# Tiles of full depth for three small products, and bundles joined, in an attention and feed-forward kernel

## The chip, the cores and the metric

The kernel runs on one core of one Trainium2 chip. The metric is the device time of one execution in microseconds; smaller is better. Each of the core's engines (PE for matrix products, DVE and ACT for work on vectors, POOL as their helper, SP for issuing DMAs) takes its instructions strictly in the order in which the program lists them, and waits at an instruction whose operands are not there.

## The reference

Attention with landmarks (Nystrom), 8 batches, 8 heads, 576 tokens, 64 columns a head, then a feed-forward block whose input is mixed by a Fourier transform:

```python
q_lm = q.reshape(B, H, 32, 18, D).mean(axis=3);  k_lm = the same of k
A, Bm, C = sm(q, k_lm), sm(q_lm, k_lm), sm(q_lm, k)      # sm: softmax of scale * a @ b.T
Z = Bm.T / (norm1(Bm) * norminf(Bm) + 1e-6)
for _ in range(6): Z = 2 * Z - Z @ Bm @ Z
x = heads side by side of A @ Z @ C @ v                   # 576 x 512 a batch
u = x + real(fft(fft(x, axis=1), axis=2))
un = (u - mean) / sqrt(var + 1e-6)                        # over the 512 columns
out = u + relu(un @ w_ch1) @ w_ch2                        # 512 -> 2048 -> 512
```

## The kernel before

The eight heads of a batch stand in two groups of four. The tokens of a batch are four tiles of 128 and a rest of 64, which shares a tile with the rest of the next batch. `attention(b)` writes the work of one batch; `landmarks` in it computes R = C v (32 landmark rows a head), the iteration for Z, and from both the 64 x 32 blocks W (`Wx`) and its transpose (`Wt`); `mix` makes the rows of u from A, W and the Fourier tables. Two tiles of 128 rows of un are a chunk of the feed-forward block: chunks 0 to 3 by `chunk`, the others by `seven`, a scheme with seven block products instead of eight. Numbers that need more than f16 are split into a high and a low f16 part, and a product of two such is three f16 products (`mm3`).

The parts that the change touches, each by its place on PE:

- Last queries' scores. The scores of the 64 rest queries against the landmark keys. They are the third pass (u == 2) of the loop over `aes` in `attention`. `qr[g]` holds the rest queries of group g. Group 0's scores go to PSUM rows 0 to 63 and group 1's to rows 64 to 127, in tiles of 128 x 64 of PE's array (the trace writes such a tile as 128*64: rows of depth * columns).
- Rest tokens. `rest` holds the rest's part of A, high and low, with group 0 in partitions 0 to 63 and group 1 in 64 to 127; it is multiplied by the cosine and sine table `t1t` with a depth of 64, three products a group, two groups side by side in the array (64*128 in the trace). Those six products follow the twelve for the other tokens (`at<-t,mt`) in one bundle, once for cosine and once for sine in each batch.
- Values' product. `values_turned` multiplies C transposed by v for batches from 2 (`LATE`) on; batches 0 and 1 use `values`, which stays as it is. A group has 16 f32 products of depth 128 and 4 of depth 64 in a bundle of its own, with its own PSUM bank. The 64 rows of v's fifth block are loaded twice, to the upper and the lower half of the partitions, and two heads use each half.
- W and its transpose. The transpose (two products, `at<-row,R`) is in one bundle, then its absolute sum `wm` is taken and summed over partitions by a product with `ones` (in `pow2`), and W (eight products, `at<-R,row`) is a second bundle in another bank.

What sets the order: the code doesn't issue instructions; `Order.op` records them with an assumed cost, and `Order.solve` deals them to the engines in simulated time, one list for each engine. PE work between `together()` and `apart()` is a bundle: it stays in one piece. Attention comes ahead of the feed-forward work where its operands are ready, and the feed-forward work fills what is left. PSUM banks and SBUF slots are given out by the same dealing. All instructions carry the line of the one call that issues them, L1307 in the profile, so groups are told apart by the names of tiles: `hp` and `acc` are the feed-forward banks, `at` the banks for everything else (the seven-product scheme also keeps two of them), `big`, `mt`, `ml`, `row`, `sum` and `h` are slots in SBUF.

Of the kernel before, what the change touches and what calls it, by code (L numbers as in the profile page):

```python
# [11 lines left out]
F16 = mybir.dt.float16  # L12
# [4 lines left out]
ALU = mybir.AluOpType  # L17
AX = mybir.AxisListType

P = 128  # L20
# [3 lines left out]
SEG = 73  # L24
# [61 lines left out]
IN_ORDER = ("u", "big", "ml", "mt", "unT", "h", "ws", "sum", "hp", "acc")  # L86
KEEP = ("at", "row")
LINK, PATIENCE = 0.05, 0.0
# [80 lines left out]
class Op:  # L169
    __slots__ = ("engine", "calls", "held", "took", "phase", "group", "margin", "seq", "before", "after", "tiles", "claims", "rank", "start", "end", "nbytes", "port", "name", "other", "urgent")  # L170


class Order:
# [21 lines left out]
    def op(self, engine, held, took, writes, reads, call, nbytes=0, port=False):  # L195
        o = self.bundle if engine == "PE" and self.bundle else None
        if o is None:
            o = Op()
            o.engine, o.calls, o.held, o.took, o.seq = engine, [], 0.0, 0.0, len(self.ops)
            o.phase, o.group, o.margin, o.nbytes, o.port = self.phase, self.group, self.margin, nbytes, port  # L200
            o.other, o.urgent = {}, False
# [12 lines left out]

    def touch(self, o, v, write):
# [19 lines left out]
    def solve(self):  # L235
# [10 lines left out]
        free = dict.fromkeys(engines, 0.0)  # L246
        pipe, port, now, done = 0.0, 0.0, 0.0, []
        self.done = done
# [57 lines left out]
        while events:  # L306
# [22 lines left out]
            for e in [e for e in best if e not in again] + again:  # L329
# [17 lines left out]
                o.start = now  # L347
                free[e] = now + o.held
                if o.port:
# [71 lines left out]
class Kernel:  # L421
# [95 lines left out]
    def mm(self, out, a, b, start=True, stop=True, share=1.0):  # L517
        n, m = math.prod(b.shape[1:]), math.prod(a.shape[1:])
        if a.dtype != F32:
            held = max(0.02, 0.003 + n / 2400 * share + (0.01 if share < 1.0 or 100 < n < 200 else 0.0))  # L520
        else:
            held = max(0.2, 0.02 + 4 * n / 2400) * (m / 128 if m < 128 else 1.0) * share
        self.order.op(
            "PE", held * self.cold, 0.2, [out], [a, b],
            (self.nc.tensor, "matmul", (out, a, b), {"start": start, "stop": stop, "skip_group_check": True}),
        )
        self.order.ops[-1].name = "mm"

    def tr(self, out, a, ident):
        self.order.op("PE", 0.21 * self.cold, 0.2, [out], [a, ident], (self.nc.tensor, "transpose", (out, a, ident), {}))  # L530
        self.order.ops[-1].name = "tr"

    def mm3(self, out, a, b, start=True, stop=True, share=1.0):
# [124 lines left out]
    def attention(self, b):  # L658
# [9 lines left out]
        NQ = 16 * SEG  # L668
# [33 lines left out]
        qm = [h[:, 0:2048].rearrange("p (y r t) -> p y r t", y=2, r=2) for h in qhs]  # L702
        qr = [h[:, 2048:2304].rearrange("p (y r t) -> p y r t", y=2, r=2) for h in qhs]
        for g in range(2):
            qs = loads[g][1][:, 0:NQ].rearrange("p (x t) -> p x t", t=2 * SEG)
            for t, a, w in ((qm[g], 1, 128), (qr[g], 129, 16)):
                split(
                    *(t[:, y].rearrange("p r (s t) -> p (r s) t", t=w) for y in range(2)),
                    qs[:, :, a : a + w], sc[:, g : g + 1],
                )  # L710
# [9 lines left out]
        for u in range(3):  # L720
# [4 lines left out]
            self.together()  # L725
            for j in range(4) if u < 2 else range(2):
                rows, at, g = (slice(0, P), 128 * j, u) if u < 2 else (slice(64 * j, 64 * j + 64), 0, j)
                for pr in range(2):
                    mm3(ps[rows, at : at + 128].rearrange("p (h r m) -> p h r m", h=2, r=2)[:, :, pr],
                        lambda y: qm[g][:, y, pr, 128 * j : 128 * j + 128] if u < 2 else qr[g][:, y, pr],  # L730
                        lambda y: kbd[:, g, y, pr, :])
            self.apart()
# [13 lines left out]
        for u in range(3):  # L746
# [4 lines left out]
            av = ae.rearrange("p (h m) -> p h m", m=32)  # L751
            if u == 2:
                rest = self.small([P, 2, 128], "rest", F16, bufs=1)
# [3 lines left out]
            else:  # L757
                self.A.copy(hy[:, :, 0], av)
                self.E.tensor_tensor(hy[:, :, 1], av, hy[:, :, 0], ALU.subtract)
            self.turn(AT, hl)  # L760
            ATs.append(AT)
            if u == 2:
                Fs.append(rest)
                break
# [13 lines left out]
        for x in range(2):  # L778
# [124 lines left out]
    def values_turned(self, loads, T, ci, R):  # L903
        V, mm = self.V, self.mm
        ET = self.big()[:, 0 : 2 * S]
        for a, b in ((0, 640), (640, 2 * S)):
            self.E.tensor_tensor(ET[:, a:b], T[:, a:b], T[:, 2 * S + a : 2 * S + b], ALU.add)
        E = ET.rearrange("p (c m) -> p c m", m=P)
        low, high = slice(0, 64), slice(64, P)
        for g in range(2):  # L910
            vf = loads[g][2].rearrange("p (c d) -> p c d", c=5)
            ps = self.at()
            self.together()
            tiles = [(0, low, 4, 4)] + [(x, slice(0, P), 5 * x + c, c) for c in range(4) for x in range(2)] + [(1, high, 4, 4)]
            for x, rows, blk, c in tiles:
                for r in range(2):
                    i, at = 2 * r + x, 64 * g + 32 * r
                    mm(ps[32 * i : 32 * i + 32, 0:64], E[rows, blk, at : at + 32], vf[rows, c, 64 * i : 64 * i + 64],
                       (x, c) in ((0, 4), (1, 0)), (x, c) in ((0, 3), (1, 4)))
            self.apart()  # L920
            V.tensor_scalar(R[:, g], ps[:, 0:64], ci[:, g : g + 1], 2.0**-14, ALU.mult, ALU.mult)

    def landmarks(self, b, loads, qbd, lm):
# [73 lines left out]
        for g in range(2):  # L997
# [3 lines left out]
            )  # L1001
        pst = self.at()
# [3 lines left out]
        self.apart()  # L1006
        self.order.ops[-1].before.update(self.used[1])
        self.used[1] = {}
        wm = small(1, "wm")
        V.tensor_reduce(wm, pst[:, 0:128], AX.X, ALU.add, apply_absolute_value=True)  # L1010
        count = len(self.order.ops)
        ew, rw = self.pow2(wm, 1, "wx")
        total = self.order.ops[count]
        total.urgent = True
        ps = self.at()
        self.together()
        for g in range(2):
# [5 lines left out]
        self.apart()  # L1023
        self.order.ops[-1].before[total] = None
        self.order.ops[-1].before.update(self.used[0])
        self.used[0] = {}
        sc = small(3, "scw")
# [3 lines left out]
        Wx, Wt = self.Wx, self.Wt  # L1031
        for W, src in ((Wt, pst[:, 0:128]), (Wx, ps[:, 0:256])):
            self.split(*(W[:, y].rearrange("p a b -> p (a b)") for y in range(2)), src, sc[:, 0:1])
# [341 lines left out]
```

## Time and profile before

| | us |
|---|---|
| median of 3 runs | 965.05 (964.23 to 967.74) |
| the profiled execution | 965.58 |
| its span | 963.4 |
| PE busy | 911.0 (95%), 10510 matmuls |
| DVE, ACT, POOL busy | 760.1, 482.8, 216.5 |
| mean granted clock of PE | 0.979 |

A row of the timeline gives the start, the duration and the count of instructions of one kind in a row; matmuls overlap, so the time a row takes on PE is the difference of two starts. Each f32 product stands as two records. Shapes of a matmul are tile of the array, output, type: `64*32 64x64 f32` is a depth of 64 and 32 columns of the array, 64 columns streamed. A bracket at the end of a row is the idle time ahead of it and who ended it.

### The profile page before, as it was taken

Reading aid. Unit: us, or ns where it says so; the run is one execution under the profiler, and the core shown is the slowest. Engines: PE = TensorE matmul, PEld = TensorE weight load, DVE = VectorE, ACT = ScalarE, POOL = GpSimd, SP = SyncE. Lnnn points to the kernel's source line nnn. Section 1 sums busy time; section 2 is a strip of 40 time slices with the busy share of each in tenths; the row PEclk is TensorE's granted clock in tenths of the full one; section 3 lists DMA queues with packets and bytes.
Section 4 is the critical chain, followed back from the end, with each engine's and each line's share of the span. In section 5 each row is a group of like instructions: output and inputs, shape, how many; then the busy total and the mean of one; then the engine's idle time right before and its main releaser. Section 6 shows DMA issues by size and latency. Waiting matters only on the chain. (4 is left out here: it accounts for less than half of the span.)

```text
span 963.4 us, 26055 instructions
## 1 busy us (share of the span) xinstructions
PE 911.0 (95%) x10510; PEld 731.0 (76%) x10510; DVE 760.1 (79%) x2016; ACT 482.8 (50%) x1007; POOL 216.5 (22%) x250
## 2 busy tenths in 40 slices
PE   5767999999999999999999999999999999999997
PEld 3546667666666788888887778887888878888886
DVE  7989996898898769887789886996698858665455
ACT  5999842355455445454454444545345533333332
POOL 0211210153643213321223002242031303101010
PEclk9768999999999999999999999999999999999999
DMA  9966110734737433556252733467235522435231
GB/s 350 355 226 178 41 37 13 182 105 95 258 90 189 157 89 104 155 124 213 67 155 88 195 104 89 133 130 216 67 100 154 132 74 73 120 112 117 82 105 50
DMA packets 161993, 128.23 MB, mean 133 GB/s; under 512 B 80080, under 2 KB 150736, under 8 KB 161744
## 3 DMA queue, kind: packets, MB, share of 16 engines
q1 hardware_dynamic: 161872, 126.57, 45.3%
q8 instruction: 82, 1.34, 0.6%
q14 instruction: 39, 0.32, 0.1%
HBM read 94.15 MB, written 14.68 MB: 113 GB/s over the span
## 5 line engine op out<-in xcount | busy, mean ns | idle before, releaser
L1307 PE MATMUL hp<-unT,w 128*128 128x256 f16 x3264 | 388.5, 273 | 10.3 <-DMA unT<-row 8.9
L1307 PEld LDWEIGHTS <-w 128*128 128x128 f16 (+1 forms) x3584 | 345.0, 99 | 68.5 <-issue 10.4
L1307 PEld LDWEIGHTS <-h 128*128 128x128 f16 x2604 | 247.2, 98 | 61.9 <-issue 6.6
L1307 PE MATMUL acc<-w,h 128*128 128x256 f16 (+1 forms) x1260 | 198.6, 294 | 1.1 <-DVE u L1307 0.4
L1307 DVE TENSOR_TENSOR sum<-ws 128x256 f32<-128x256 f32 (+1 forms) x278 | 99.8, 405 | 69.9 <-ACT ws L1307 68.1
L1307 ACT ACTIVATE ws<-hp 128x512 f32<-128x512 f32 x112 | 66.6, 595 | 140.1 <-PE hp L1307 139.9
L1307 ACT CAST h<-sum 128x640 f16<-128x640 f32 x112 | 81.1, 724 | 82.6 <-DVE sum L1307 68.1
L1307 PE MATMUL at<-big,h 128*128 128x256 f16 x672 | 110.1, 273 | 0.0
L1307 POOL TENSOR_TENSOR sum<-ws 128x256 f32<-128x256 f32 (+1 forms) x58 | 41.3, 727 | 252.9 <-ACT ws L1307 197.9
L1307 DVE TENSOR_TENSOR h<-sum,h 128x640 f16<-128x640 f32 x79 | 65.0, 823 | 19.2 <-ACT h L1307 18.0
L1307 POOL TENSOR_TENSOR h<-sum,h 128x640 f16<-128x640 f32 x33 | 46.4, 1405 | 150.3 <-ACT h L1307 150.3
L1307 ACT CAST row<-row 128x256 f16<-128x256 f32 (+1 forms) x76 | 36.7, 505 | 40.4 <-DVE row L1307 32.2
L1307 DVE TENSOR_REDUCE lm<-big 128x32 f32<-128x576 f32 (+1 forms) x48 | 44.3, 946 | 14.7 <-DMA big<-k_dram 8.1
L1307 PE MATMUL at<-w,h 128*128 128x256 f16 x336 | 55.0, 273 | 0.0
L1307 PE MATMUL acc<-big,h 128*128 128x256 f16 x336 | 55.0, 273 | 0.0
L1307 PEld LDWEIGHTS <-big 128*128 128x128 f16 (+1 forms) x768 | 40.8, 104 | 11.0 <-issue 5.0
L1307 ACT CAST h<-ws 128x256 f16<-128x256 f32 x112 | 45.3, 404 | 2.7
L1307 DVE SCALAR_TENSOR_TENSOR u<-at,scw,row 128x128 f32<-128x128 f32 (+3 forms) x120 | 39.0, 386 | 3.7 <-PE at L1307 3.5
L1307 DVE TENSOR_TENSOR h<-ws,h 128x256 f16<-128x256 f32 x95 | 40.5, 426 | 0.0
L1307 ACT ACTIVATE big<-big 128x1168 f16<-128x1168 f32 (+1 forms) x26 | 25.3, 983 | 29.2 <-DMA big<-q_dram 21.7
L1307 PEld LDWEIGHTS <-mt 64*128 64x128 f16 (+1 forms) x752 | 28.6, 98 | 14.5 <-issue 8.0
L1307 DVE SCALAR_TENSOR_TENSOR u<-acc,winv,u 128x512 f32<-128x512 f32 x50 | 35.3, 741 | 3.0 <-PE acc L1307 2.7
(223 smaller groups left out, 1254.7 us busy)
## 6 DMA issues: line engine op xcount, KB each, us to landing
big<-sums SPq DMA_DIRECT2D x336, 128.0 KB, 2.2
w<-w_dram SPq DMA_DIRECT2D x22, 512.0 KB, 8.1
big<-q_dram SPq DMA_DIRECT2D x16, 584.0 KB, 6.2
big<-k_dram SPq DMA_DIRECT2D x16, 576.0 KB, 4.8
out_dram<-u SPq DMA_DIRECT2D x36, 256.0 KB, 2.2
big<-v_dram SPq DMA_DIRECT2D x12, 512.0 KB, 4.8
big<-w_dram SPq DMA_DIRECT2D x10, 512.0 KB, 6.5
sums<-row SPq DMA_DIRECT2D x40, 128.0 KB, 2.5
```

The lines of the kernel that those rows point to most:

```text
L1307: getattr(engine, name)(*map(real, args), **{k: real(x) for k, x in kw.items()})
```

## The change

Four edits to products, and one to the planner:

1. Last queries' scores: `qr` gets twice the columns, with group g's queries in its own half of 64 and zeros in the other (16 memsets on POOL in all). Both groups' products then use the full 128 x 128 tile and are summed in the same PSUM rows.
2. Rest tokens: `rest` holds, for a group, the high part in one half of the partitions and the low part in the other, and `t1t` holds the same rows in both halves; two products of depth 128 a group take the place of three of depth 64. On ACT two copies become one cast and four copies of 64 partitions.
3. Values' product: both groups in one bundle and one bank, 40 products, all of depth 128. The fifth block of v is loaded by columns: the heads of one parity have their 64 rows in the upper partitions, the other in the lower, and zeros beside them, which the padded input holds. That is three DMAs a group for it instead of two.
4. W and its transpose: one bundle, one bank; the absolute sum is taken behind both.
5. The planner adds 0.095 (`SWITCH`) to PE's assumed time where the tile of the array changes, and assumes less for narrow f32 products. This changes the order alone.

```diff
+    def mode(self, mode):
+        o = self.ops[-1]
+        if o.modes and o.modes[-1] != mode:
+            o.held += SWITCH
+            o.took += SWITCH
+        o.modes.append(mode)
...
-                for x in range(2):
-                    self.dma(to[64 * x : 64 * x + 64, 4], src[0:64, 4])
+                of = lambda t, x: t[:, 4].rearrange("p (r x d) -> p r x d", r=2, x=2)[:, :, x]
+                self.dma(of(to, 0), of(src, 0))
+                for half in range(2):
+                    self.dma(of(to, 1)[64 * half : 64 * half + 64], of(src, 1)[64 - 64 * half : 128 - 64 * half])
...
+            self.G.memset(qr[g][..., 64 - 64 * g : 128 - 64 * g], 0.0)
...
-                rows, at, g = (slice(0, P), 128 * j, u) if u < 2 else (slice(64 * j, 64 * j + 64), 0, j)
+                    at, g = (128 * j, u) if u < 2 else (0, j)
...
-                self.A.copy(rest[:, 0], ae)
-                self.E.tensor_tensor(rest[:, 1], ae, rest[:, 0], ALU.subtract)
-                self.A.copy(hy, rest.rearrange("p y (h m) -> p h y m", m=32))
+            self.A.copy(hy[:, :, 0], av)
+            self.E.tensor_tensor(hy[:, :, 1], av, hy[:, :, 0], ALU.subtract)
...
+                    self.A.copy(rest[own, g], hy[own, :, 0])
+                    self.A.copy(rest[other, g], hy[own, :, 1])
...
-            for ya, yb in ((0, 0), (0, 1), (1, 0)):
-                for g in range(2):
-                    rows = slice(64 * g, 64 * g + 64)
-                    mm(pss[g][:, 0:320], Fs[2][rows, ya], self.t1t[rows, x, yb, :], False, ya == 1, 0.5)
+            for g in range(2):
+                for y in range(2):
+                    mm(pss[g][:, 0:320], Fs[2][:, g], self.t1t[:, x, y, :], False, y == 1)
...
+        for c in range(5):
+            for g in range(2):
+                for i in range(4):
+                    at = 64 * g + 32 * (i // 2)
+                    blk = c if c == 4 else 5 * (i % 2) + c
+                    mm(ps[32 * i : 32 * i + 32, 64 * g : 64 * g + 64], E[:, blk, at : at + 32], vf[g][:, c, 64 * i : 64 * i + 64],
+                       c == 0 and g == 0, c == 4)
...
-            mm(pst[64 * g : 64 * g + 64, 0:128], R[:, g], nbd[:, g, :, 0:32])
-        self.apart()
...
+            mm(pst[64 * g : 64 * g + 64], R[:, g], nbd[:, g, :, 0:32])
         for g in range(2):
             for i in range(4):
```

The built lists show it. On PE, the values' product of batch 2 before: behind a step of the iteration (`ES`), a bundle for each group (`big`, the slots of C transposed and v; `at`, two banks):

```order
L1307 LDWEIGHTS w_110
L1307 MATMUL hp_106<-big_69,w_110 128x256
L1307 MATMUL at_105<-ES_165 32x64 x8
L1307 MATMUL at_103<-big_64,big_67 32x64 x20
L1307 MATMUL at_104<-big_65,big_67 32x64 x20
L1307 LDWEIGHTS sum_100
L1307 MATMUL acc_108<-w_111,sum_100 128x512
```

And after, its last rows (ten rows of four, two groups by turns, into one bank):

```order
L1319 MATMUL at_105<-big_66,big_65 32x64 x4
L1319 MATMUL at_105<-big_64,big_65 32x64 x4
L1319 MATMUL at_105<-big_66,big_65 32x64 x4
L1319 LDWEIGHTS h_94
L1319 MATMUL acc_108<-w_111,h_94 128x512
```

The two bundles of 20 have become one of 40, away from the iteration's step and between products of the feed-forward block.

On PE, W in batch 0 before, where `acc_108<-w_110` is a product of the weights with themselves that the kernel uses for scales:

```order
L1307 LDWEIGHTS w_110
L1307 MATMUL acc_108<-w_110 128x128
L1307 MATMUL at_103<-row_82,R_139 64x128 x2
L1307 MATMUL at_104<-wm_166,ones 128x1
L1307 MATMUL at_105<-R_139,row_82 64x64 x8
```

After:

```order
L1319 MATMUL at_103<-wm_204,ones 128x1
L1319 LDWEIGHTS w_110
L1319 MATMUL acc_108<-w_110 128x128
L1319 MATMUL at_102<-row_82,R_139 64x128 x2
L1319 MATMUL at_102<-R_139,row_82 64x64 x8
L1319 MATMUL at_104<-wm_166,ones 128x1
```

The sum `wm_166` has moved behind both products, which now share a bank.

On ACT in batch 0, the copies of the rest before (`ae`, the rest's part of A; `hl`, what is sent to be transposed; `w` and `ws`, weights being split):

```order
L1307 ACTIVATE w_110<-w_111 128x512 x2
L1307 CAST rest_184<-ae_178 128x128
L1307 ACTIVATE w_110<-w_111 128x512
L1307 CAST mt_74<-mt_78 128x512
L1307 COPY hl_182<-rest_184 128x256
L1307 ACTIVATE w_110<-w_111 128x512 x3
L1307 ACTIVATE Wt<-at_103,scw_172 128x128
L1307 CAST mt_78<-mt_75 128x512
L1307 ACTIVATE Wx<-at_105,scw_172 128x256
```

After:

```order
L1319 ACTIVATE w_110<-w_111 128x512 x3
L1319 CAST hl_182<-ae_178 128x4x32
L1319 CAST mt_74<-mt_78 128x512
L1319 COPY rest_184<-hl_182 64x128 x4
L1319 ACTIVATE w_110<-w_111 128x512 x3
L1319 CAST mt_78<-mt_75 128x512
L1319 ACTIVATE ws_97<-w_110,wsa 128x512
L1319 ACTIVATE Wt<-at_102,scw_172 128x128
L1319 ACTIVATE Wx<-at_102,scw_172 128x256
```

Four short copies have come in, and a step of the weights stands ahead of W's split. Further down, three more weight steps (`ACTIVATE w`) stand ahead of the first row's cast for the feed-forward block than before.

More of the change, by code (lines that the diff above doesn't have):

```diff
@@ L86 @@
 IN_ORDER = ("u", "big", "ml", "mt", "unT", "h", "ws", "sum", "hp", "acc")
-KEEP = ("at", "row")
+KEEP, SWITCH = ("at", "row"), 0.095
 LINK, PATIENCE = 0.05, 0.0
@@ L169 @@
 class Op:
-    __slots__ = ("engine", "calls", "held", "took", "phase", "group", "margin", "seq", "before", "after", "tiles", "claims", "rank", "start", "end", "nbytes", "port", "name", "other", "urgent")
+    __slots__ = ("engine", "calls", "held", "took", "phase", "group", "margin", "seq", "before", "after", "tiles", "claims", "rank", "start", "end", "nbytes", "port", "name", "other", "urgent", "modes")
 class Order:
@@ L246, in solve @@
         free = dict.fromkeys(engines, 0.0)
-        pipe, port, now, done = 0.0, 0.0, 0.0, []
+        pipe, port, now, done, mode = 0.0, 0.0, 0.0, [], None
         self.done = done
@@ L347, in solve @@
                 o.start = now
+                if o.modes:
+                    if o.modes[0] != mode:
+                        o.held += SWITCH
+                        o.took += SWITCH
+                    mode = o.modes[-1]
                 free[e] = now + o.held
@@ L526, in mm @@
         )
+        size = lambda v: 128 if v > 64 else 64 if v > 32 else 32
+        self.order.mode((size(a.ap.ap[0][1]), size(m)))
         self.order.ops[-1].name = "mm"
@@ L531, in tr @@
         self.order.ops[-1].name = "tr"
+        self.order.mode((128 if a.ap.ap[0][1] > 64 else 64, 128))
     def mm3(self, out, a, b, start=True, stop=True, share=1.0):
@@ L725, in attention @@
             self.together()
[L726 to L729 removed]
+            for pr in range(2):
+                for j in range(4) if u < 2 else range(2):
+                    at, g = (128 * j, u) if u < 2 else (0, j)
+                    mm3(ps[:, at : at + 128].rearrange("p (h r m) -> p h r m", h=2, r=2)[:, :, pr],
                         lambda y: qm[g][:, y, pr, 128 * j : 128 * j + 128] if u < 2 else qr[g][:, y, pr],
[L731 removed]
+                        lambda y: kbd[:, g, y, pr, :], u < 2 or j == 0, u < 2 or j == 1)
             self.apart()
@@ L762, in attention @@
             if u == 2:
-                Fs.append(rest)
+                rest = self.small([P, 2, 4, 32], "rest", F16, bufs=1)
+                for g in range(2):
+                    own, other = (slice(64 * i, 64 * i + 64) for i in (g, 1 - g))
+                    self.A.copy(rest[own, g], hy[own, :, 0])
+                    self.A.copy(rest[other, g], hy[own, :, 1])
+                Fs.append(rest.rearrange("p g h m -> p g (h m)"))
                 break
@@ L908, in values_turned @@
         E = ET.rearrange("p (c m) -> p c m", m=P)
-        low, high = slice(0, 64), slice(64, P)
-        for g in range(2):
[L911 to L919, printed above, removed]
-            self.apart()
-            V.tensor_scalar(R[:, g], ps[:, 0:64], ci[:, g : g + 1], 2.0**-14, ALU.mult, ALU.mult)
+        vf = [loads[g][2].rearrange("p (c d) -> p c d", c=5) for g in range(2)]
+        ps = self.at()
+        self.together()
+        for c in range(5):
+            for g in range(2):
+                for i in range(4):
[3 more added lines that the diff above has]
+                       c == 0 and g == 0, c == 4)
+        self.apart()
+        for g in range(2):
+            V.tensor_scalar(R[:, g], ps[:, 64 * g : 64 * g + 64], ci[:, g : g + 1], 2.0**-14, ALU.mult, ALU.mult)
     def landmarks(self, b, loads, qbd, lm):
@@ L1001, in landmarks @@
             )
-        pst = self.at()
+        ps = self.at()
+        pst = ps[:, 256:384]
         self.together()
         for g in range(2):
-            mm(pst[64 * g : 64 * g + 64, 0:128], R[:, g], nbd[:, g, :, 0:32])
[L1006 to L1016, printed above, removed]
+            mm(pst[64 * g : 64 * g + 64], R[:, g], nbd[:, g, :, 0:32])
         for g in range(2):
@@ L1023, in landmarks @@
         self.apart()
-        self.order.ops[-1].before[total] = None
-        self.order.ops[-1].before.update(self.used[0])
-        self.used[0] = {}
+        for used in self.used:
+            self.order.ops[-1].before.update(used)
+            used.clear()
+        wm = small(1, "wm")
+        V.tensor_reduce(wm, pst, AX.X, ALU.add, apply_absolute_value=True)
+        count = len(self.order.ops)
+        ew, rw = self.pow2(wm, 1, "wx")
+        self.order.ops[count].urgent = True
         sc = small(3, "scw")
```

21 lines of the change are left out of this document (8 added, 13 removed).

## The prediction

> **What bounds the kernel now.** I read the page first, then the windows of the span, then TensorE's waits, then its timeline where the change falls.
>
> ```profile
> PE 911.0 (95%) x10510; PEld 731.0 (76%) x10510; DVE 760.1 (79%) x2016; ACT 482.8 (50%) x1007; POOL 216.5 (22%) x250
> PE   5767999999999999999999999999999999999997
> PEclk9768999999999999999999999999999999999999
> ```
>
> TensorE (PE) is busy 911.0 of 963.4 us; from the fifth slice on nothing but nines, at the full granted clock. Windows (busy us of PE, PEld, DVE, ACT, POOL; clock, DMA share, GB/s):
>
> ```profile
> 0.00:50.00 50.00, 30.68 (x439) 21.35 (x440) 42.55 (x134) 38.44 (x83) 6.31 (x12) 0.86 1.04 355
> 50.00:100.00 50.00, 35.16 (x366) 29.25 (x364) 45.01 (x102) 48.09 (x94) 6.91 (x8) 0.76 0.63 198
> 300.00:500.00 200.00, 200.00 (x2407) 167.28 (x2405) 160.95 (x428) 96.29 (x199) 52.69 (x60) 1.00 0.46 131
> 500.00:700.00 200.00, 193.97 (x2426) 162.54 (x2425) 159.65 (x429) 93.65 (x198) 48.50 (x54) 1.00 0.47 132
> ```
>
> In the first 100 us PE stands idle for 34 us, because ACT and DVE are nearly full (48.09 and 45.01 of 50). Later it hardly stands, because matmuls of the feed-forward layer fill every hole of the attention. So there a microsecond of PE work removed is a microsecond of the end, and a microsecond added to ACT, DVE, POOL or SP costs nothing unless PE, which takes its instructions in order, stands for it. The waits that do exist (total, times, longest):
>
> ```profile
> PE hp L1307 <- DMA unT<-row: 8.9, 1, 8.9
> PE at L1307 <- DVE big L1307: 5.1, 5, 2.7
> ```
>
> **What a change of tile costs.** Three products of 256 columns, the same again, then a product in 32x32 tiles, on PE's timeline (start, us):
>
> ```profile
> 409.99 0.49 PE L1307 MATMUL at<-big,h 128*128 128x256 f16 x3
> 410.31 0.49 PE L1307 MATMUL at<-w,h 128*128 128x256 f16 x3
> 410.74 0.33 PE L1307 MATMUL at<-ES 32*32 32x32 f32 x16
> ```
>
> From start to start three take 0.32 us (0.108 each) when the next row keeps the 128x128 tile, and 0.43 when it doesn't. So a change into a smaller tile costs about 0.10 us. The way out shows at the rest tokens:
>
> ```profile
> 661.06 0.99 PE L1307 MATMUL at<-t,mt 128*128 128x160 f16 x12
> 661.99 0.58 PE L1307 MATMUL at<-t1t,rest 64*128 64x320 f16 x6
> 662.50 1.49 PE L1307 MATMUL hp<-unT,w 128*128 128x256 f16 x12
> ...
> 110.03 1.47 PE L1307 MATMUL acc<-w,mt 128*128 128x512 f16 x6
> 111.34 0.38 PE L1307 MATMUL at<-nrm,ones_bd 128*128 128x128 f32 x2
> ```
>
> Products of 160 columns take (0.93 - 0.10) / 12 = 0.069, of 256 columns 0.108, of 512 columns 1.31 / 6 = 0.218: one line, 0.426 ns a column, so 320 columns are 0.136. The six half-depth products run as three pairs, 0.41; the row takes 0.51, so the way out costs 0.10 too. The Trainium skill has this (TensorEngine Tiling (Array Packing), Key Properties: changing the tiling mode drains the engine) without a price; the trace gives it, 0.10.
>
> **The parts on PE.**
>
> Rest tokens, 16 bundles (8 batches, cosine and sine). Before 0.10 + 0.51 = 0.61. After, 4 x 0.136 = 0.545 and no change of tile, since the products before them have 128x128 tiles. Gain 0.065 x 16 = 1.0 us; an error of 0.01 a product moves it by 0.6, so 0.4 to 1.7. This is where the skill speaks against the change: the same page (Theoretical Speedup) gives a depth of 64 or less up to twice the rate in two row tiles. By that alone, three pair times become four, and this part would lose 16 x 0.136 = 2.2 us; the time would be 961.6. The pairs do show in the row (0.51 for six); the two changes around them, 0.20, take it back.
>
> Last queries' scores, 8 bundles of 12 (the first row pair is the other queries', 24 products of the same columns in the full tile):
>
> ```profile
> 733.35 0.86 PE L1307 MATMUL at<-kbd,big 128*128 128x64 f16 x24
> 734.05 0.49 PE L1307 MATMUL at<-w,h 128*128 128x256 f16 x3
> ...
> 740.87 0.47 PE L1307 MATMUL at<-kbd,big 128*64 128x64 f16 x12
> 741.27 0.94 PE L1307 MATMUL hp<-unT,w 128*128 128x256 f16 x7
> ```
>
> Full tile: 0.70 / 24 = 0.029 each, so 12 x 0.029 = 0.35 against 0.10 + 0.40. Gain 0.15 x 8 = 1.2; 0.8 if half of them stand beside another small tile, where one change stays.
>
> Values' product, batches 2 to 7 (each f32 product is two records; the last row is batch 1's older form, 16 products of full depth and 4 of half; the row after it, at 110.03, stands above):
>
> ```profile
> 664.19 1.95 PE L1307 MATMUL at<-big,big 64*32 64x64 f32 x80 [0.21 <-DVE big L1307]
> 666.07 1.16 PE L1307 MATMUL hp<-unT,w 128*128 128x256 f16 x9
> ...
> 552.62 1.12 PE L1307 MATMUL at<-big,big 64*32 64x64 f32 x40
> 553.67 0.50 PE L1307 MATMUL at<-big,h 128*128 128x256 f16 x3
> ...
> 109.20 0.90 PE L1307 MATMUL at<-big,ml 128*32 128x64 f32 x40
> ```
>
> Both groups in a row take 1.88 with four changes inside and one at the end, plus 0.10 ahead: 1.98 a batch. A group alone takes 1.05 + 0.10, two of them 2.30. In the order, four batches have them in a row and two apart. After: 40 products, one change ahead, one behind. Price of one, from the pair: (1.88 - 0.50) / 40 = 0.0345; from batch 1: (0.83 - 0.20) / 20 = 0.0315. The second is nearer in shape; 40 of them and 0.20 are 1.46, by the first 1.58. I take 1.5: gain 4 x 0.48 + 2 x 0.80 = 3.5 us (3.0 to 3.8).
>
> W and its transpose, 8 batches:
>
> ```profile
> 560.13 0.44 PE L1307 MATMUL at<-row,R 128*64 128x128 f32 x4
> 560.50 0.83 PE L1307 MATMUL acc<-w,h 128*128 128x256 f16 x6
> ...
> 565.09 0.74 PE L1307 MATMUL at<-R,row 128*64 128x64 f32 x16 [0.67 <-DVE wx_e L1307]
> 565.76 0.50 PE L1307 MATMUL acc<-w,h 128*128 128x256 f16 x3
> ```
>
> 0.37 and 0.67, each with a change on both sides. In one bundle a way in and a way out go: 0.20 x 8 = 1.6; 1.5, since one stood beside another small tile; at least 1.2.
>
> Sum on PE: 1.0 + 1.2 + 3.5 + 1.5 = 7.2 us (ends 5.4 to 8.3). A count checks it: walking through the tiles of both built programs I find 373 changes of tile before and 283 after. 90 x 0.10 = 9.0, less the longer rest products (16 x (0.545 - 0.41) = 2.2) and scores (8 x 0.05 = 0.4), plus the values' shorter ones (6 x 40 x 0.003 = 0.7): 7.1.
>
> **What it adds elsewhere.** ACT: two copies a batch become one cast and four copies of 64 partitions. Nearest rows, and the weight steps that now stand ahead:
>
> ```profile
> 32.17 0.20 ACT L1307 COPY ES<-at 128x64 f32<-128x64 f32 x1
> 33.96 0.28 ACT L1307 CAST rest<-ae 128x128 f16<-128x128 f32 x1
> 36.10 0.40 ACT L1307 COPY hl<-rest 128x256 f16<-128x256 f16 x1
> 36.41 1.79 ACT L1307 ACTIVATE w<-w 128x512 int32<-128x512 uint32 x3
> ```
>
> Four at 0.20 to 0.28 and one at 0.28, less 0.28 and 0.40: 0.4 to 0.7 more a batch. From batch 1 on ACT is half idle (93.65 of 200) and PE has the feed-forward work to go on with: nothing. In batch 0 ACT is full and PE waits 8.9 us for the first unT, so it counts there: 0.6. Also, three more weight steps (1.8 us) come ahead of the first row's cast in the new order; they are only moved, so the loss is between nothing and 1.8. I take none of it, since the weights finish that much sooner and the first chunk needs both; the end is 0.6 + 1.8 = 2.4.
>
> W's absolute sum now follows the 8 products of Wx too, 0.67 later; its scales and both splits wait behind it, and the product with t2 for them. PE fills that with the cosine and sine products or the feed-forward: nothing. If that cover failed, 0.67 a batch. The bundle also waits for the last product with the old Wx, which stands ahead of it on PE anyway.
>
> DMA and POOL: the values' fifth block comes in three pieces instead of two, 12 issues more on SP (the memset of the unused half of the last queries is 16 more on POOL, which is busy 48.5 of 200).
>
> ```profile
> L1307 SPq DMA_DIRECT2D big<-v_dram x40: 379/527/1376, 3.8 to 734.5; - x40
> ```
>
> At 0.527 us an issue a batch's SP queue is 1.1 us longer; what stands behind are sums units and transposes. The DMA engines are busy 0.46 of the time: nothing; uncovered, 1.1 in six batches.
>
> The order: the planner now counts 0.095 for a change of tile, so PE's row is dealt anew nearly everywhere. That removes no work. Its price is waits, below.
>
> Forecast: 7.2 - 0.6 = 6.6 us. The profiled execution took 965.58 (span 963.4 and 2.2 around it), 0.5 above the median of the three runs, 965.05. 965.05 - 6.6 = 958.4.
>
> **Rivals.** A measurement of this kernel tells about 0.5%, 4.8 us, from no change: 960.2 to 969.9.
>
> 1. The waits at the merged places go too. The 5.1 us of waits for DVE big stand there: the values' rows (0.21 above, and two longer ones) and this one, W's transpose behind a DVE that waits for a load:
>
> ```profile
> 671.02 1.42 DVE L1307 TENSOR_REDUCE lm<-big 128x32 f32<-128x576 f32 x2 [2.73 <-DMA big<-q_dram]
> ...
> 675.02 0.44 PE L1307 MATMUL at<-row,R 128*64 128x128 f32 x4 [2.74 <-DVE big L1307]
> ```
>
> If all go, 958.4 - 5.1 = 953.3. For it: a new order, with changes of tile counted. Against: a load that is late stays late.
>
> 2. The first chunk starts late. From the first unT on, PE is full, so its delay comes one for one. The three weight steps and the four copies, with the DVE work that waits for them, could make it 5 us instead of 0.6: 962.8. It is "no change" from 2.4 us on and slower only past 12. For it: ACT's 48.09 of 50. Against: the moved work returns.
>
> 3. Slower: the new order sets attention products on PE closer to what DVE makes, and PE, in order, stands like at 675 us. A wait of that kind is 2.74; five more than now (13.7) turn it into 972.1, and slower is decided from 11.5 us, between four and five. For it: such waits exist, and loads are still issued by one SP queue. Against: from 300 to 700 us only 6.0 are idle (200.00 and 193.97 of 200 in the windows), and PE has feed-forward rows to hand.
>
> 4. Weight loads are exposed. The fuller tiles load 128 rows where half-depth tiles could load beside each other.
>
> ```profile
> L1307 PEld LDWEIGHTS <-w 128*128 128x128 f16 (+1 forms) x3584 | 345.0, 99 | 68.5 <-issue 10.4
> ```
>
> 64 rest and 96 score products with 0.099 each in the open would be 15.8 us: 974.2. Against: 24 full-tile scores take 0.70, 0.029 each, loads included. The Trainium skill (TensorE: Matmul & The Clock Gate, Part 3) states that a weight load overlaps with running matmuls only when its row group differs; by that rule this rival would come, and the scores' row speaks against it.
>
> That the change doesn't do what it says is settled by the order: the bundles are merged, 90 changes fewer. Only their price could fail, and it shows in three rows.
>
> **How the numbers follow.** Forecast (955.5 to 960.2): 0.50. Rival 1: 0.14. Rival 2: 0.24. Rival 3: 0.10. Rival 4: 0.02. Faster by over 0.5%: 0.50 + 0.14 = 0.64; within: 0.24; slower: 0.12. The range reaches down to where the best sum meets rival 1 (965.05 - 8.3 - 5.1 = 951.7) and up to rival 2 with one new wait (962.8 + 2.74 = 965.5) and a part of rival 3: 952 to 967. Outside stay most of rivals 3 and 4 and the far end of 1, under 0.2.
>
> **What the new profile would show.** Right: PE busy about 7 us less; the rest tokens as 128*128 128x320 rows, four in 0.55; one values' row a batch of 80 records in about 1.4 to the next row; scores at 0.03 each in one form; W's two shapes side by side; the first feed-forward row at 77 to 78 us. Wrong: rest products well over 0.14, or 64-column ones over 0.04 (rival 4); the wait for unT past 11 us (rival 2); PE's waits for DVE big, ES, mt or row grown by over 5 us after 172 us (rival 3).

## Result, and the profile after

The change made the kernel slower. It took 977.81 us (median of 4 runs, 974.57 to 981.8); the kernel before took 964.64 on the same chip. The ratio, over undisturbed runs only and so not quite the quotient of the medians, is 1.0115 (95% interval 1.0081 to 1.015). I had forecast 958.4. The profiled execution took 974.57, with a span of 972.8. It is the fastest of the four, at a mean granted clock of 0.973 against 0.967 to 0.971 in the others; so the profile shows some 9 of the 13 us between the medians.

Engines, PE by slice and the granted clock by slice, from the page of the kernel after:

```profile
PE 908.0 (93%) x10478; PEld 734.3 (75%) x10478; DVE 768.7 (79%) x2022; ACT 488.2 (50%) x1031; POOL 221.4 (23%) x260
PE   4666899999999999999999899999999999999997
PEclk9767999999999999999999999999999999999999
```

PE is busy 3.0 us less, and the span is 9.4 longer: PE stands more. The windows tell where (same columns as before):

```profile
0.00:50.00 50.00, 26.76 (x424) 19.68 (x424) 42.28 (x130) 37.66 (x82) 4.82 (x12) 0.83 1.03 352
50.00:100.00 50.00, 34.70 (x366) 27.03 (x344) 45.06 (x108) 46.99 (x93) 8.76 (x11) 0.73 0.59 189
100.00:172.00 72.00, 68.31 (x801) 44.75 (x799) 58.40 (x175) 38.47 (x85) 14.74 (x15) 0.98 0.09 26
300.00:500.00 200.00, 196.62 (x2361) 164.26 (x2359) 160.63 (x431) 96.04 (x205) 43.26 (x49) 1.00 0.50 131
500.00:700.00 200.00, 193.87 (x2404) 164.57 (x2402) 168.80 (x444) 94.85 (x203) 52.86 (x59) 1.00 0.48 132
```

The third window of the kernel before:

```profile
100.00:172.00 72.00, 70.65 (x826) 45.14 (x825) 60.84 (x181) 35.91 (x79) 11.61 (x12) 1.00 0.07 18
```

Where nothing stood between 300 and 500 us, 3.4 us stand now. Ahead of 172 us PE is busy 6.7 us less (3.9, 0.5 and 2.3 in the three windows), at a lower clock in each.

The products themselves cost what was forecast, or less. PE's timeline after: rest tokens, last queries' scores, W and its transpose, values, each with the row behind it:

```profile
150.94 0.71 PE L1319 MATMUL at<-t1t,rest 128*128 128x320 f16 x4
151.48 0.99 PE L1319 MATMUL at<-t,mt 128*128 128x160 f16 x12
...
135.26 0.52 PE L1319 MATMUL at<-kbd,big 128*128 128x64 f16 x12
135.62 1.46 PE L1319 MATMUL acc<-w,h 128*128 128x512 f16 x6
...
139.60 0.44 PE L1319 MATMUL at<-row,R 128*64 128x128 f32 x4
139.87 0.70 PE L1319 MATMUL at<-R,row 128*64 128x64 f32 x16
140.50 1.47 PE L1319 MATMUL acc<-w,h 128*128 128x512 f16 x6
...
660.12 1.32 PE L1319 MATMUL at<-big,big 128*32 128x64 f32 x80
661.37 0.50 PE L1319 MATMUL acc<-w,h 128*128 128x256 f16 x3
```

From start to start: 0.54 (0.61 before), 0.36 (0.50), 0.90 for W's two (0.37 + 0.67 and one change of tile more), and 1.25 for both groups' values (1.88, or 2.10 apart).

To see the rest I use one number of my own, **standing time**: the clock time at a point of the trace, less the full-clock work of PE's row up to there. The work is the sum, over the row, of what each kind of product takes from start to start in the two traces (by tile, type, columns and the row behind it, after 180 us). Standing time so holds waits and half-clock time. Work is 885.3 us before and 880.6 after. Standing by a given time, us:

| | 100 | 172 | 350 | 800 | 945 |
|---|---|---|---|---|---|
| before | 53.7 | 54.8 | 62.1 | 71.8 | 71.6 |
| after | 57.0 | 62.7 | 75.1 | 86.2 | 85.9 |

So 4.7 us of work went and 14.3 of standing came: 7.9 by 172 us, 5.1 more by 350, 1.4 more to 800. The split hangs on how the kinds are formed. Formed by the shapes of a product and of the next one, with starts behind a wait left out, work is 888.0 before and 881.1 after: 6.9 went and 16.4 came. Both counts agree on where it came.

### The profile page after: what moved, and what is told of

The parts are those of the page before. It is cut to its first block, busy times and chain, and to the rows that moved or that the text cites. A ratio compares the mean times of both kernels' runs of the same rounds, so it can differ in the third digit from the quotient of the medians.

```text
span 972.8 us, 26055 instructions
## 1 busy us (share of the span) xinstructions
PE 908.0 (93%) x10478; PEld 734.3 (75%) x10478; DVE 768.7 (79%) x2022; ACT 488.2 (50%) x1031; POOL 221.4 (23%) x260
## 4 chain that ended last, share of the span: by engine, by line
PE 65%; DVE 15%; ACT 7%; DMA 6%; issue 4%; POOL 2%; SPq 1%; DVEq 0%; ACTq 0%; POOLq 0%
PE hp L1319 29%; PE at L1319 19%; PE acc L1319 16%; DMA big<-big 2%; DVE row L1319 2%; DVE u L1319 2%; DMA big<-q_dram 2%; ACT w L1319 2%; DVE h L1319 1%; DVE mt L1319 1%; ACT row L1319 1%; DVE big L1319 1%; ACT h L1319 1%; ACT big L1319 1%; ACT ws L1319 1%
## 5 line engine op out<-in xcount | busy, mean ns | idle before, releaser
L1319 DVE TENSOR_TENSOR sum<-ws 128x256 f32<-128x256 f32 (+1 forms) x277 | 104.0, 421 | 72.6 <-ACT ws L1319 69.9
L1319 POOL TENSOR_TENSOR sum<-ws 128x256 f32<-128x256 f32 (+1 forms) x59 | 43.4, 750 | 288.8 <-ACT ws L1319 225.9
L1319 ACT CAST row<-row 128x512 f16<-128x512 f32 (+1 forms) x76 | 36.8, 505 | 38.3 <-DVE row L1319 25.0
L1319 DVE SCALAR_TENSOR_TENSOR row<-at,scw,row 128x262 f32<-128x262 f32 (+1 forms) x48 | 21.6, 485 | 20.0 <-ACT row L1319 19.7
```

The lines of the kernel that those rows point to most:

```text
L1319: getattr(engine, name)(*map(real, args), **{k: real(x) for k, x in kw.items()})
```

## Experiments

Each of the five sets below was timed on a chip of its own, in 3 rounds against the kernel before. Its median was 965.1, 966.5, 965.6, 966.7 and 966.4 us there and 964.6 beside the changed kernel, so a difference across sets can be off by up to 2 us. The kernels hold the old and the new version of each part, and a line of numbers says from which batch on the new one counts (99: never). PLAN stands for the cost of a change of tile, HELD for the new price of narrow f32 products; up to e7 HELD goes with PLAN. PRICE multiplies the attention products' prices from batch 2 on. "Sum" is the planner's own total for PE. The values' edit exists from batch 2 on alone, in the changed kernel too. Results together (time: median; standing by 172 us, from 172 to 800, from 800 to 945). Standing is that of the profiled execution, which in after, e10, e17 and e18 was 2 to 3 us faster than the median:

| run | edits from batch | costs | sum | us | ratio, interval | standing |
|---|---|---|---|---|---|---|
| before | none | old | 913.6 | 965 | | 54.8, 17.0, -0.2 |
| after | 0 | new | 925.4 | 977.8 | 1.0115, 1.0081 to 1.015 | 62.7, 23.5, -0.3 |
| e1 | 0 | old | 914.8 | 967.8 | 1.0025, 1.001 to 1.004 | 57.3, 23.2, -0.1 |
| e2 | none | new | 932.5 | 974.9 | 1.0104, 1.0069 to 1.0139 | 57.6, 23.9, -0.2 |
| e3 | 2 | new from 2 | 923.4 | 967.9 | 1.0022, 1.0006 to 1.0039 | 56.3, 23.5, -0.3 |
| e4 | 2 | old | 914.5 | 957.8 | 0.9918, 0.9892 to 0.9944 | 56.3, 13.7, -0.3 |
| e5 | 2, rests 0 | old | 914.8 | 962.5 | 0.995, 0.9933 to 0.9967 | 57.1, 17.5, -0.3 |
| e6 | 2, scores 0 | old | 914.5 | 958.1 | 0.9915, 0.9893 to 0.9937 | 56.7, 13.8, -0.3 |
| e7 | 2, W 0 | old | 914.5 | 962.4 | 0.9961, 0.9948 to 0.9974 | 54.7, 18.2, -0.2 |
| e8 | 2 | change of tile from 2 | 934.2 | 966.2 | 0.9999, 0.9987 to 1.0012 | 55.7, 23.9, -0.3 |
| e9 | 2 | the same, PRICE 0.832 | 914.8 | 953.4 | 0.9864, 0.9843 to 0.9884 | 55.5, 10.0, 0.0 |
| e10 | 2 | old, PRICE 1.168 | 934.2 | 971.5 | 1.0051, 1.0032 to 1.0069 | 55.4, 25.5, -0.2 |
| e11 | 2 | narrow f32 from 2 | 903.5 | 953.0 | 0.9857, 0.9836 to 0.9878 | 56.1, 9.7, 0.2 |
| e12 | 2 | old, margin 2.2 | 914.5 | 969.5 | 1.0036, 1.0018 to 1.0053 | 56.3, 24.0, 0.5 |
| e13 | 0 | old, PRICE 0.906 | 903.7 | 966.2 | 0.9989, 0.9973 to 1.0004 | 57.3, 11.1, 10.0 |
| e14 | 2 | old, margin 1.8 | 914.5 | 963.0 | 0.9962, 0.9944 to 0.998 | 56.3, 17.8, -0.2 |
| e15 | none | old, PRICE 0.906 | 902.6 | 973.6 | 1.0063, 1.0042 to 1.0085 | 56.5, 23.7, 0.2 |
| e16 | 2 | old, PRICE 0.906 | 903.4 | 961.9 | 0.9941, 0.9921 to 0.9961 | 57.0, 11.0, 5.9 |
| e17 | 0 | old, PRICE 0.906 in 2 to 4 | 909.3 | 964.5 | 0.998, 0.9963 to 0.9997 | 59.2, 15.3, -0.1 |
| e18 | 0 | new, PRICE 0.832 | 907.4 | 972.0 | 1.0053, 1.0032 to 1.0074 | 62.2, 18.4, -0.1 |

The work is 879.2 to 880.6 in every kernel with the edits, and 884.6 to 885.3 in every one without. Nearly all the rest is the order.

**First set: the edits against the costs.** The line of numbers, e1 to e4:

```diff
-SCORES, RESTS, VALUES, WS, PLAN = 0, 0, 2, 0, 0       # the changed kernel
+SCORES, RESTS, VALUES, WS, PLAN = 0, 0, 2, 0, 99      # e1
+SCORES, RESTS, VALUES, WS, PLAN = 99, 99, 99, 99, 0   # e2
+SCORES, RESTS, VALUES, WS, PLAN = 2, 2, 2, 2, 2       # e3
+SCORES, RESTS, VALUES, WS, PLAN = 2, 2, 2, 2, 99      # e4
```

> The four edits with the planner's old costs (no 0.095 for a change of tile). 278 changes of tile instead of 373 before. Theory A (the new costs deal a worse order, the edits themselves gain): about 959, PE's waits as before. Theory B (the edits in batch 0 make the first chunk late and the rest follows): 970 to 978, first unT wait ends past 80 us. Theory C (any new dealing of the early part loses, whatever caused it): also 968 to 980, with idle PE time in the first 150 us some 5 us more than before.

> The planner's new costs alone, no edit to any product (371 changes of tile). Theory A: 972 to 982, slower than with the edits by the 5 to 7 us that they gain. Theory B: 965, as before. Theory C: 968 to 980, with more idle PE time in the first 150 us.

> All edits and the new costs, but from batch 2 on alone; the order of the first 180 us or so is the old one (297 changes of tile). Theory A: 963 to 970, since the new costs go on to deal waits. Theories B and C: the early loss is gone; 958 to 962 if the waits after 172 us also follow from the early order, 964 to 968 if they come of the new dealing itself (about 7 us).

> All edits from batch 2 on alone, with the old costs (298 changes of tile). Theory A: 959 to 960. Theory B: 959 to 961. Theory C: between 957 and 968, as the dealing of batches 2 to 7 falls; the gain on PE is three quarters of 7 us plus the values' part, some 6 us.

Measured 967.8, 974.9, 967.9 and 957.8. The edits from batch 2 on gain 7.3 us (before to e4) and 7.0 (e2 to e3). The new costs lose 9.8 (before to e2), 10.0 (e1 to after) and 10.1 (e4 to e3). Taking the edits into batches 0 and 1 loses 10.0 (e4 to e1) and 9.9 (e3 to after). So from batch 2 on the total is as forecast, and two things that should cost next to nothing lose 20 between them. Theory A has e2 and e3 right and e1 wrong by 9; theory B falls with e2; theory C (any new dealing of the early part loses) comes nearest.

**Second set: which early edit, which cost.** From e4, one number each (in e8, PLAN 2 with HELD 99):

```diff
-SCORES, RESTS, VALUES, WS, PLAN = 2, 2, 2, 2, 99
+SCORES, RESTS, VALUES, WS, PLAN = 2, 0, 2, 2, 99      # e5
+SCORES, RESTS, VALUES, WS, PLAN = 0, 2, 2, 2, 99      # e6
+SCORES, RESTS, VALUES, WS, PLAN = 2, 2, 2, 0, 99      # e7
+SCORES, RESTS, VALUES, WS, PLAN = 2, 2, 2, 2, 2       # e8
```

> All four edits from batch 2 on with the old planner costs (957.8), and now the rest tokens' edit in batches 0 and 1 too. It alone adds work to ACT in the full first 100 us (one cast and four copies where two copies were). Theory ACT: this edit carries the 10 us that the early edits cost; 965 to 968, with the first unT later than 77.5 us by 1 to 2 us. Theory lot: whichever edit is added early, the rows of the first 150 us are dealt anew and lose some us each; 960 to 964, and the other two early edits lose as much. Theory neither: 957.6 (the part's own gain, 4 bundles x 0.065).

> The same base (957.8), and the last queries' scores in tiles of full depth in batches 0 and 1 too, with their memsets on POOL. Theory ACT: no work on ACT or DVE is added, so 957.5 (2 bundles x 0.15 gained). Theory lot: the row is dealt anew all the same; 960 to 964.

> The same base (957.8), and W and its transpose in one bundle in batches 0 and 1 too. Theory ACT: 957.4 (2 x 0.2 gained). Theory lot: 960 to 964. A third possibility is that the absolute sum, 0.67 us later, is not covered in the first 100 us, where PE has little else to do: then 958 to 959, with a wait for wx_e longer by under a microsecond a batch.

> All four edits from batch 2 on, the old cost of narrow f32 products, and from batch 2 on the planner counts 0.095 us for each change of tile. With both new costs it was 967.9, with both old ones 957.8. Theory tile: counting the change of tile is what deals the worse order; 966 to 970. Theory narrow: the new price of narrow f32 products does it; 957 to 959 here. Theory lot: any re-dealing of this row ends up to 10 us either way; 960 to 968, not the sum of two separate prices.

Measured 962.5, 958.1, 962.4 and 966.2. The rest tokens lose 4.7, W 4.6, the scores nothing. Theory ACT falls: W adds nothing to ACT and loses as much, and by 172 us e5 stands only 0.8 longer than e4 and e7 1.6 shorter; what they lose stands later, where no instruction of theirs differs. Counting the change of tile loses 8.4 by itself.

**Third set: pace, or the count as such, or any new dealing.** e9 and e10 edit this line (and the transposes' like it); e11 sets HELD 2 and PLAN 99; e12 the margin:

```diff
-            "PE", held * self.cold, 0.2, [out], [a, b],
+            "PE", held * self.cold * (PRICE if self.order.group >= 2 else 1.0), 0.2, [out], [a, b],
-        self.set(10 * b if b == 0 else 100 * b, b, 0.1 if b == 0 else 0.4 if b == 1 else 2.0)
+        self.set(10 * b if b == 0 else 100 * b, b, 0.1 if b == 0 else 0.4 if b == 1 else 2.2)
```

> All four edits from batch 2 on, 0.095 counted for each change of tile as in the kernel that took 966.2, but the attention products' own prices lowered by a sixth (times 0.832) from batch 2 on. The planner's sum for PE is then 914.8 us, as with the old costs (914.5, which took 957.8), and not 934.2. Theory pace: a planned PE that is slower than the real one sets attention products too close behind what DVE makes, and the sum is what matters; 957 to 960. Theory tile: counting the changes as such deals the worse order; 965 to 968. Theory lot: every new dealing ends somewhere, 953 to 968, and the sum says nothing.

> The mirror: all four edits from batch 2 on, no cost for a change of tile, but the attention products' prices raised by a sixth (times 1.168) from batch 2 on, so that the planner's sum for PE is 934.2 us as with the cost of the change. Theory pace: 965 to 968. Theory tile: 957 to 959. Theory lot: 953 to 968.

> All four edits from batch 2 on and only the new, lower price of narrow f32 products from batch 2 on, without the cost of a change of tile. The planner's sum for PE falls to 903.5 us. Theory pace: the attention products then stand further behind DVE, so no more waits than at 957.8; 953 to 958. If both new costs lose by themselves: 960 or more. Theory lot: 953 to 968.

> All four edits from batch 2 on, old costs, and the planner's distance between a DVE result and the product that reads it 2.2 us instead of 2.0 from batch 2 on. The sum for PE stays 914.5; the row is dealt anew with slightly more room. Theory pace: 956 to 958.5. Theory lot: the kernel at 957.8 was a lucky order, and a harmless re-dealing loses 3 us or more; 960 to 966.

Measured 953.4, 971.5, 953.0 and 969.5. Theory tile falls (though e9 and e10 overshoot the ranges of Theory pace): with the change counted and the sum kept, e9 is 12.8 faster than e8, and e10 slows down without counting it. PE's waits for DVE big after 172 us (total, times, longest), in e10:

```profile
PE at L1393 <- DVE big L1393: 9.0, 6, 2.7
```

and in e9:

```profile
PE at L1393 <- DVE big L1393: 1.2, 1, 1.2
```

In e10 they stand at two places that the prediction had named, W's transpose and the values' row:

```profile
243.69 0.44 PE L1393 MATMUL at<-row,R 128*64 128x128 f32 x4 [2.68 <-DVE big L1393]
...
324.66 1.32 PE L1393 MATMUL at<-big,big 128*32 128x64 f32 x80 [2.58 <-DVE big L1393]
```

That is rival 3, and I read it so: to a planner whose PE is slow, DVE's result seems in time sooner in PE's row, and the chip's PE gets there first. The rows show the waits; that the planned pace put them there is inferred. But e12 spoils the simple theory. More room should have helped, and it lost 11.7, by waits of another kind. Its windows:

```profile
225.00:250.00 25.00, 20.20 (x247) 12.64 (x247) 19.51 (x44) 8.34 (x22) 9.95 (x11) 0.93 0.42 90
250.00:275.00 25.00, 21.82 (x236) 15.15 (x234) 20.83 (x50) 12.39 (x31) 9.73 (x13) 1.00 0.73 242
```

PE's timeline in them:

```profile
243.16 2.72 PE L1392 MATMUL hp<-unT,w 128*128 128x256 f16 x12 [2.87 <-DVE h L1392]
...
268.52 1.47 PE L1392 MATMUL hp<-unT,w 128*128 128x256 f16 x12 [3.17 <-DVE h L1392]
```

and DVE's, ahead of the second wait:

```profile
264.52 1.35 DVE L1392 TENSOR_REDUCE lm<-big 128x64 f32<-128x1152 f32 x1 [3.49 <-DMA big<-k_dram]
265.79 0.76 DVE L1392 SCALAR_TENSOR_TENSOR ml<-at,ml 128x262 f16<-128x262 f32 x2
266.47 1.40 DVE L1392 TENSOR_REDUCE lm<-big 128x32 f32<-128x576 f32 x2
267.79 0.68 DVE L1392 SCALAR_TENSOR_TENSOR h<-hp,h 128x512 f16<-128x512 f32 x1
```

DVE takes its row in order too. It stands 3.49 us for a load of k, goes through the five instructions of the first three rows, and only then makes the h that frees PE's next feed-forward product, 3.17 us late. So the feed-forward isn't always there to fill a hole, as I had assumed; it needs DVE as well.

**Fourth set: is it pace, or chance?** PRICE 0.906 in e13, e15 and e16 on the edits' lines of e1, before and e4; margin 1.8 in e14.

```diff
-PRICE = 1.0
+PRICE = 0.906
```

> All four edits in every batch (967.8 with the old costs), no cost for a change of tile, and the attention products' prices lowered by a tenth (times 0.906) from batch 2 on; the planner's sum for PE is 903.7 us instead of 914.8. Theory pace: the 10 us that the edits in batches 0 and 1 seemed to cost were waits of the row dealt later, at 225 to 350 us, and most of them go: 954 to 960. Theory early: the first 150 us themselves cost them (a later first unT, work on ACT), and the lower price can't return them: 962 to 966. Theory lot: 953 to 970.

> The counterpart of the margin of 2.2 us (969.5): all four edits from batch 2 on, old costs, margin 1.8 instead of 2.0 (957.8). Theory of two waits (a larger margin draws feed-forward products ahead, and they wait for DVE's h; a smaller one sets attention products close behind DVE's big): 960 to 968, with waits for DVE big and few for DVE h before hp. Theory pace alone (room only helps): 958 to 962. Theory lot: 953 to 970, with either kind of wait.

> The kernel before, without any edit, with the attention products' prices times 0.906 from batch 2 on (planner's sum 902.6 instead of 913.6). Theory pace: a gain as with the edits, 959 to 963; the edits are then worth 6 to 8 us at this pace too. Theory lot: 953 to 970; and if it is 955 or less, the edits are worth nothing once the order is good.

> All four edits from batch 2 on, no cost for a change of tile, all attention prices times 0.906 from batch 2 on: the same planner's sum (903.4) as with the lower price of narrow f32 products alone (903.5, which took 953.0), spread otherwise. In this plan PE stands 5.4 us between 700 and 900 us. Theory pace: 952 to 956; if the sum alone is too coarse and it matters which product is priced lower, 957 to 962. Theory lot: 953 to 970.

Measured 966.2, 963.0, 973.6 and 961.9. e15 refutes pace as a general law: its sum falls by 11, and it loses 6.9 to the kernel before in its own set. Between 172 and 800 us the lower price did work where the edits are in: 11.1 (e13) against 23.2 (e1), 11.0 (e16) against 13.7 (e4). Then both lose it at the end, where the feed-forward has run out ahead of the last batch's unT; e13:

```profile
837.58 9.35 PE L1393 MATMUL hp<-unT,w 128*128 128x256 f16 x60 [7.34 <-DMA unT<-row]
```

So in these two attention set early waits in the middle, and attention set late waits at the end. The margins don't bear that out: e14's time lies in the range of the theory of two waits, but it waits for DVE h (3.9 us ahead of hp, 2.2 ahead of acc) and only 1.4 for DVE big, the reverse of what I expected. In e13 the early edits' loss is gone by 800 us (68.4 of standing against 80.5 in e1; e16, at the same price without the early edits, has 68.0): it isn't a price of batches 0 and 1, but of the row that was dealt behind them.

**Fifth set: the middle without the end, and the changed kernel's own pace.** e17 ends the lower price at batch 5; e18 is the changed kernel with PRICE 0.832.

```diff
-            "PE", held * self.cold * (PRICE if self.order.group >= 2 else 1.0), 0.2, [out], [a, b],
+            "PE", held * self.cold * (PRICE if 2 <= self.order.group < 5 else 1.0), 0.2, [out], [a, b],
```

> All four edits in every batch, no cost for a change of tile, attention prices times 0.906 in batches 2 to 4 only, and the old ones from batch 5 on. With the lower price to the end (966.2) the trace showed 68.4 us of PE's time without work by 800 us, 12 less than with the old price (80.5), and then a wait of 7.3 us for the last unT, in a plan whose PE stands 7.6 us there; in this plan it stands nowhere. Theory two sides (too early: waits in the middle; too late: no feed-forward work is left at the end): the middle stays good and the tail's wait goes; 955 to 960. Theory early (edits in batches 0 and 1 cost 10 in the first 150 us): 964 or more. Theory lot: 953 to 970.

> The changed kernel itself (977.8: four edits in every batch, both new costs in every batch), with the attention products' prices times 0.832 from batch 2 on; the planner's sum for PE is 907.4 us instead of 925.4. Batches 0 and 1 keep the new costs' order. Theory two sides: what the changed kernel lost after 172 us (23 us of standing PE against 17 before) falls to 10 or less, and its loss in the first 150 us (8 us more than before) stays; 961 to 967. Theory lot: 953 to 978. If the loss of the first 150 us is made good later anyway: 955 to 960.

Measured 964.5 and 972.0, both outside the theory's range. In e17 the end's wait went, but PE is idle for 5.5 us between 650 and 800 us (1.0 in e13), half of it ahead of this row:

```profile
672.74 1.32 PE L1393 MATMUL at<-big,big 128*32 128x64 f32 x80 [2.73 <-DVE big L1393]
```

In e18 the standing after 172 us falls by 5 of 23, not by 13, and its first 172 us stay as bad as the changed kernel's, as expected. "Every new dealing ends somewhere" covers both.

**What is settled, and what isn't.** Four kernels with the same edits and sums of 914.5 to 914.8, e9, e4, e14 and e12, take 953.4, 957.8, 963.0 and 969.5: 16 us between dealings of the same products. A dealing is more than an order: it also splits work between DVE and its helper POOL, and DVE runs 2024, 2014, 1997 and 2035 instructions in the four. With that spread the 7.3 and 7.0 of the first set don't measure the edits; the 4.7 to 6.9 us of work do. Raising the attention's planned time, by the new costs or by PRICE, lost in all five pairs (before to e2, e1 to after, e4 to e3, to e8 and to e10: 8.4 to 13.6). Lowering it gained in five (after to e18, e1 to e13 and to e17, e8 to e9 and, by the narrow price, e4 to e11: 1.6 to 12.8) and lost in two (e4 to e16, before to e15: 4.1 and 6.9). So the new costs' loss is a tendency, with a mechanism that e10's rows suggest; the changed kernel's own rows don't show it, since its waits for DVE big after 172 us didn't grow (next section). How much of the changed kernel's 10 is tendency and how much the dealing's chance, these runs don't tell. Nor do they tell whether some order with all edits in batches 0 and 1 is as good as e9's. e11, 953.0, and e9 are the fastest: the edits from batch 2 on with one new cost each (and PRICE 0.832 in e9), 1.4% under the kernel before.

## Why the prediction was wrong, point by point

**The step that failed** is one sentence: the order "is dealt anew nearly everywhere. That removes no work. Its price is waits", which I then put at nothing, with 0.10 and 0.24 for waits of two kinds. The price is 14.3 us of standing, and a new dealing alone moves this kernel by up to 16. With a spread like that no sum of 6.6 could carry a chance of 0.64. The ground for "nothing", that feed-forward products fill every hole, failed with it: from 172 to 900 us PE's waits rose from 10.5 to 16.1 us, and over half of the rise is feed-forward products that wait for DVE's h (2.5 us before, 5.7 now). Why this dealing is a bad one among many stays open.

**The prices on PE** held: the rows above have 0.54, 0.030 a score, 0.90 and 1.25, where I had 0.545, 0.029, 1.04 less a change, and 1.4. Taken row by row as in the forecast, with a change of 0.10 ahead of each small tile, the four parts come to 16 x 0.07 + 8 x 0.14 + 8 x 0.24 + (4 x 0.63 + 2 x 0.95) = 8.6 us, over the 7.2; the kind-by-kind work shows 4.7 less, 5.3 in e4, and 6.9 by the other count. So part of the difference is the counting; all have the sign and the order of size. By the Trainium skill (TensorEngine Tiling (Array Packing), Theoretical Speedup) alone, the rest tokens would have lost an estimated 2.2 us for giving up their row tiles. Their row is 0.54 against 0.61, so the changes around the pairs outweighed them.

**The first chunk** (rival 2) came in part. I had 0.6 for ACT and the first feed-forward row at 77 to 78 us; it stands at 81.35:

```profile
80.45 0.61 PE L1319 MATMUL acc<-w 128*128 128x128 bf16 x4 [9.57 <-DVE w L1319]
81.35 2.72 PE L1319 MATMUL hp<-unT,w 128*128 128x256 f16 x12 [0.29 <-DMA unT<-row]
...
112.15 0.42 PE L1319 MATMUL at<-ident,ml 128*64 128x128 f32 x1 [2.42 <-DVE nrm L1319]
112.36 2.77 PE L1319 MATMUL hp<-unT,w 128*128 128x256 f16 x12
...
117.85 1.47 PE L1319 MATMUL hp<-unT,w 128*128 128x256 f16 x12
```

The long wait there was 8.9 us for unT before. Now it is 9.57 us for a part of the weights from DVE, and unT comes 0.29 us behind; what made both later isn't shown. By 100 us 3.3 are lost, and a wait for nrm with a half-clock stretch behind it (last section) makes most of the rest of 7.9. The copies are a small part at most: in e5, the early edit that brings them, the first feed-forward row is 1.6 us later than in e4 (79.15 against 77.52), but standing by 172 us only 0.8 longer, near my 0.6. e2, without any edit, stands 2.8 longer than the kernel before by 172 us, e1, with all of them and the old costs, 2.5; both causes together make 7.9, more than their sum.

**New waits** came too, but not those of rival 3. The wait that I had quoted, before W's transpose at 675 us, is gone, and the sign that I had set, waits for DVE big, ES, mt or row grown by over 5 us after 172 us, didn't show: 6.3 us before, 7.0 now. Others grew, for h, u and Wx. From 172 to 900 us (total, times, longest), before and after:

```profile
PE at L1307 <- DVE big L1307: 4.9, 4, 2.7
PE hp L1307 <- DVE h L1307: 2.5, 2, 1.4
...
PE at L1319 <- DVE big L1319: 4.7, 6, 1.6
PE acc L1319 <- DVE h L1319: 3.7, 2, 3.2
PE hp L1319 <- DVE h L1319: 2.0, 1, 2.0
PE at L1319 <- DVE u L1319: 1.6, 3, 1.1
```

My grounds against it, PE idle only 6.0 of 400 us, showed that the old order fitted DVE, not that any order would. In the tight stretch DVE has little slack to give (e9, the good order, 25 us wide):

```profile
225.00:250.00 25.00, 25.00 (x315) 17.93 (x314) 22.58 (x59) 11.51 (x31) 11.87 (x14) 1.00 0.62 163
250.00:275.00 25.00, 24.53 (x285) 16.65 (x283) 25.00 (x64) 12.96 (x30) 16.15 (x21) 1.00 0.57 187
```

DVE is busy for 22.58 and then for all 25.00 us, while PE is idle for only 0.47. A row of PE that is set nearer to DVE would have to stand there; that is argued from these rows, not shown by them.

**Right:** weight loads in the open (rival 4) didn't come; 12 full-tile scores take 0.36, loads included. (A slip in the prediction: the last of PE's forty slices is a 7, not a nine.)

## What to carry to other kernels

When an edit also re-deals a planner's row, price the new deal as a term of its own: deal the same work a few ways (here margins of 1.8, 2.0 and 2.2 spread by 11.7 us, and with e9 by 16) and take the spread as the error of every forecast and of every comparison of two versions. A true price for one kind of instruction, added to a plan whose other prices had been fitted without it, can make the plan worse (e8); in the one pair that tried it, keeping the plan's total took the loss back (e9). The busy share of the bottleneck says how well the present order fits, not how much another one may shift.

## What the hardware showed beyond that

A short wait can cost more than itself. Behind the 2.42 us for nrm above, twelve products of 256 columns take 2.77 us instead of 1.47. In e12 the row behind a wait of 2.87 takes 2.72 (its window's mean clock is 0.93), and the row behind a longer one, 3.17, takes 1.47. Length doesn't decide it: a wait of 3.22 us in e1 (it ends at 651.6) meets such a stretch, one of 3.22 in the changed kernel (at 540.7) doesn't. A half-clock stretch of the former kind lasts 3.4 us in the clock's records, so at half speed it costs 1.7 us of work; all stretches ahead of a trace's end are multiples of that (3.4, 6.8, 10.2, 13.7, 17.1, 20.5, 23.9). The Trainium skill (TensorE: Matmul & The Clock Gate, Part 1: The HAM clock gate) gives a free-running activity window of about 3.4 us; the stretches agree with it, and a window that doesn't start with the wait would explain why the 2.87 is hit and the 3.17 isn't, though no run here shows the window itself.
